# Attention and two dense stages on one core: the first batch's dense steps in two rounds of five inner blocks

## The chip, the cores and the metric

The kernel runs on one core of a Trainium2 chip. The metric is the device time of one execution, in microseconds; lower is better. Times of several executions are given by their median. Five engines run their own instruction streams in order and wait for each other by semaphores: TensorE (PE, matrix products and transposes), VectorE (DVE), ScalarE (ACT), GpSimd (POOL), and SyncE (SP), which here only issues DMA transfers.

## The reference, cut to what matters

```python
def _attn_ref(q, k, v, tau):                 # (4, 8, 576, 64) each
    scores = scale * np.matmul(q, k.transpose(0, 1, 3, 2))
    thresh = np.max(scores, axis=-1, keepdims=True) - tau
    scores = np.where(scores >= thresh, scores, -1000000000.0)
    attn = np.exp(scores - np.max(scores, axis=-1, keepdims=True))
    attn = attn / (np.sum(attn, axis=-1, keepdims=True) + 1e-09)
    return np.matmul(attn, v)
...
x = attn_out.transpose(0, 2, 1, 3).reshape(2304, 512)
h = x @ w_in                                 # moe: (512, 2048)
g = np.where(h >= 1, h, np.where(h <= -1, 0.0, (h + 1) ** 2 / 4))
x = g @ w_out                                # (2048, 512)
h = x @ w_in2                                # moe2
out = (h * np.clip(h + 3.0, 0.0, 6.0) / 6.0) @ w_out2
```

The result is compared in float32.

## The kernel before, in words

**Attention.** There are 16 jobs, one for each batch (4) and pair of heads (4); job j belongs to batch j // 4. A job has five blocks of 128 query rows (the last of 64) and one block is one step t of `attention()`, 80 steps in all. A step computes scores of two heads into two PSUM banks pairs, P0 and P1 (L285); VectorE reads them, negates them and finds the row maximum (L297); ScalarE takes the exponential (L301); VectorE applies the threshold and sums (L307). A step later TensorE transposes the result (L245, banks Q0, Q2 or Q3), ScalarE copies it to SBUF as `Gf` and `Gt` (L328, L342), and TensorE multiplies it with v (L362). Blocks 2, 3 and 4 of a job also hold the norm of the job before (L395 to L403) and the transposes of the next q and k (L257, L268), which take turns in the banks P0 and P1. The page's line L301 has nine instructions for each job, so the first of each nine marks a job's start.

**Dense stage 1 beside attention.** When the four jobs of batch 0 are done (in job 4, whose step t is 23), `dense1` begins to give out steps in the gaps of attention: for groups g of 256 tokens (two for each batch, six in all) and inner blocks f of 128, ten of the sixteen (NF1 = 10), a step n computes h for (g, f) (`em_h`, 12 products, L486; then ScalarE L495, L496, VectorE L497, ScalarE L503, GpSimd L504) and one or two parts of the outer product for an earlier step (`em_part`, 6 products each, L543, bank Q3). All matrices are split into a high and a low part of reduced float32, and three products are taken for each. `split_x` loads a group's activations (`xst`) and splits them (L469 on ScalarE, L470 on VectorE). The other six inner blocks follow after attention (L528), then stage 2.

**Weight conversions.** The dense weights come as 64-bit numbers and are converted in the kernel, 512 KB a block: 20 blocks (10 of w_in, 10 of w_out) are needed for `dense1`. A conversion has two halves. `split_a` is L111 and L114 on ScalarE, L115 on GpSimd, L122 on VectorE; `split_b` is L128 on VectorE, L130 on GpSimd, then the high part on GpSimd (L133) or, once `mode["mlp"]` is set, on ScalarE (L135), and the low part on GpSimd (L137). `Weights.prefetch` keeps three loads (`w_raw`) ahead of the conversion. From step t = 6 on, a half is emitted at each attention step, and a second at each even one; in `dense1`, `weights.upto` emits whatever is due two steps ahead by `first_use`.

**What sets the order.** A scheduler with its own clock orders each engine's instructions, moving those whose inputs are ready ahead of others; order is otherwise forced by `after(x, y)` alone, which keeps x behind y. In `split_a`, L111 is ordered behind `pins["S"]`, which is None during attention. TensorE's dense products are ordered behind the last but one attention product (`pin_mlp`).

Of the kernel before, what the change touches and what calls it, by code (L numbers as in the profile page):

```python
# [18 lines left out]
def kernel(  # L19
# [84 lines left out]
    def split_a(kind, m, f):  # L104
        t = wraw.pop((kind, m, f))
        pool = wbase if f < NF1 else wpool[f]
        hi = pool.tile([128, 512], F32R, tag=f"w{kind}h{f}", name=f"w{kind}h{f}")
        lo = pool.tile([128, 512], F32R, tag=f"w{kind}l{f}", name=f"w{kind}l{f}")
        c = stage.tile([128, 512], U32, tag="w_c", name="w_c", bufs=2)
        r = t[:, :, 0].bitcast(I32)  # L110
        x = S.activation(out=r, in_=t[:, :, 0], func=ACTF.Copy, scale=2.0 ** -29)  # L111
        after(x, pins["S"])
        if mode["att"]:
            S.activation(out=f32(c), in_=f32(t[:, :, 1]), func=ACTF.Abs)  # L114
            G.tensor_scalar(  # L115
                out=f32(c), in0=f32(c), scalar1=122879.9921875, scalar2=2.0 ** -15, op0=ALU.min, op1=ALU.max)
        else:
            S.activation(out=f32(c), in_=f32(t[:, :, 1]), func=ACTF.Abs)
            x = V.tensor_scalar(
                out=f32(c), in0=f32(c), scalar1=2.0 ** -15, scalar2=122879.9921875, op0=ALU.max, op1=ALU.min)  # L120
            after(x, pins["V"])
        V.tensor_scalar(out=c, in0=c, scalar1=3, scalar2=0x3FFFFFFF,  # L122
                        op0=ALU.logical_shift_left, op1=ALU.bitwise_and)
        wc[kind, m, f] = (hi, lo, c, t, r)
# [147 lines left out]
    def em_scores(j, i):  # L272
# [179 lines left out]
    def split_x(key, kks=range(KD)):  # L452
        m, g, ph = key
# [78 lines left out]
    def em_part(key, half, f):  # L532
# [3 lines left out]
        if f == 0:  # L536
            acc[key] = bank("Q3")
        a = acc[key]
        for i in range(2):
            c = slice((2 * half + i) * 128, (2 * half + i + 1) * 128)  # L540
            o = a[:, i * GRP:(i + 1) * GRP]
            for x, (l, r) in enumerate(((wh[:, c], gh), (wh[:, c], gl), (wl[:, c], gh))):
                mm = T.matmul(o, l, r, start=(f == 0 and x == 0 and i == 0),  # L543
                              stop=(f == NF1 - 1 and x == 2 and i == 1), skip_group_check=True)
# [4 lines left out]
        if f == NF1 - 1:  # L549
            ob = mt.tile([128, 512], F32, tag="io", name="ob", bufs=2)  # L550
            if half:
                S.activation(out=ob, in_=acc.pop(key), func=ACTF.Copy)
            else:
                V.tensor_copy(out=ob, in_=acc.pop(key))
            nc.sync.dma_start(
                out=narrow(x2p, key[1])[:, 2 * half:2 * half + 2, :],
                in_=ob.rearrange("p (k n) -> p k n", k=2))
# [34 lines left out]
    n_h = NG * NF1  # L592
    outs = [(g, half, f) for g in range(NG) for half in range(2) for f in range(NF1)]
    OFF = NF1 + 2 * MLAG - 3
    steps, o = [], 0
    while o < len(outs):
        n = len(steps)
        steps.append([])
        while o < len(outs) and (o < 2 * (n + 1) - OFF or n >= n_h) and outs[o][0] * NF1 + outs[o][2] + MLAG <= n:
# [4 lines left out]
    HOLD = 1 + max(n - g * NF1 - f for n, l in enumerate(steps) for g, half, f in l if half)  # L604

    def dense1(ready, ahead):

        for n, l in enumerate(steps[:n_h]):
            g, f = divmod(n, NF1)
            key = (0, g, 1)  # L610
            if key not in xs:
                while not ready(g):
                    yield None
                split_x(key)
            ahead(n, f)
# [221 lines left out]
```

## Time and profile before

| | us |
|---|---|
| median of 3 runs (1193.73 to 1196.18) | 1195.55 |
| the profiled execution | 1197.37 |
| its span, first to last instruction | 1195.6 |
| TensorE busy in it | 1139.7 (95%) |
| ScalarE busy | 628.8 (53%) |
| VectorE busy | 580.2 (49%) |
| GpSimd busy | 419.5 (35%) |

The shares are means over a program of several stages: attention alone, attention with dense steps from about 150 us, dense work alone from about 550 us. They say little of any one stage; the rows below cut the span by jobs.

### The profile page before, as it was taken

How to read it: one execution, taken by the hardware profiler on the slowest of the kernel's cores; microseconds unless marked ns; L12 is line 12 of the kernel's file. 1: busy time of each engine (PE TensorE's matmuls, PEld its weight loads, DVE VectorE, ACT ScalarE, POOL GpSimd, SP SyncE). 2: the span in 40 equal slices, each digit the busy share in tenths (PEclk: the TensorE clock that was granted, in tenths of full speed). 3: DMA queues.
4: the chain of work that ended last, by engine and by line, in shares of the span. 5: the costliest groups of instructions: out<-in, count | busy, mean ns of one | idle time of the engine just before them, and what ended most of it. 6: DMA issues, size and time to landing. Idle time of an engine off the chain costs nothing.

```text
span 1195.6 us, 17992 instructions
## 1 busy us (share of the span) xinstructions
PE 1139.7 (95%) x6680; PEld 908.8 (76%) x6680; DVE 580.2 (49%) x1196; ACT 628.8 (53%) x1218; POOL 419.5 (35%) x396
## 2 busy tenths in 40 slices
PE   6877789999999999999999999999999999999998
PEld 4444467776777777777888988888888888888886
DVE  4889865455565565653642675555740121121111
ACT  4677766564665665655654676654542222233222
POOL 1676621110111111112762666656742213222221
PEclk9989999999999999999999999999999999999999
DMA  4444521112211122103421244453210010010000
GB/s 119 125 126 135 146 59 40 50 42 60 61 28 39 52 59 68 30 20 112 154 89 44 85 136 158 144 166 99 89 46 12 1 58 9 1 44 2 18 1 36
DMA packets 106792, 82.45 MB, mean 69 GB/s; under 512 B 66512, under 2 KB 90576, under 8 KB 106704
## 3 DMA queue, kind: packets, MB, share of 16 engines
q1 hardware_dynamic: 105344, 81.00, 23.1%
q8 instruction: 53, 0.87, 0.3%
q10 hardware_dynamic: 1360, 0.30, 0.1%
q14 instruction: 35, 0.29, 0.1%
HBM read 63.96 MB, written 17.30 MB: 68 GB/s over the span
## 4 chain that ended last, share of the span: by engine, by line
PE 86%; DVE 5%; ACT 3%; DMA 3%; issue 1%; SPq 1%; POOL 1%; ACTq 0%; DVEq 0%; POOLq 0%
PE Q L486 34%; PE P L528 26%; PE Q L543 7%; PE Q L362 6%; PE P L285 6%; PE Q L245 5%; DVE p L297 2%; DMA w_raw<-in_moe_w_in_dram 1%; DVE p L307 1%; PE P L245 1%; ACT e L301 1%; DVE w_c L128 1%; DMA xd<-xu 1%; ACT r L495 0%; PE P L395 0%
## 5 line engine op out<-in xcount | busy, mean ns | idle before, releaser
L504 POOL TENSOR_TENSOR gl<-r,gh 128x512 fp32r<-128x512 f32 (+1 forms) x190 | 205.8, 1083 | 645.3 <-ACT gh L503 625.5
L486 PE MATMUL Q<-xh,wih 128*128 128x512 f32 (+1 forms) x760 | 265.1, 350 | 2.4 <-ACT xh L469 1.4
L486 PE MATMUL Q<-xl,wih 128*128 128x512 f32 (+1 forms) x760 | 257.8, 339 | 0.4 <-DVE xl L470 0.4
L486 PE MATMUL Q<-xh,wil 128*128 128x512 f32 (+1 forms) x760 | 257.4, 339 | 0.0
L500 DVE SCALAR_TENSOR_TENSOR r<-r,Q 128x512 f32<-128x512 f32 (+1 forms) x80 | 50.7, 633 | 248.4 <-ACT r L499 248.3
L486 PEld LDWEIGHTS Q<-xh,wih 128*128 128x128 f32 x760 | 144.6, 190 | 33.0 <-issue 10.6
L503 ACT ACTIVATE gh<-r 128x512 fp32r<-128x512 f32 (+1 forms) x190 | 99.9, 526 | 122.1 <-PE P L528 52.3
L486 PEld LDWEIGHTS Q<-xl,wih 128*128 128x128 f32 x760 | 144.5, 190 | 17.2 <-DVE xl L470 1.0
L486 PEld LDWEIGHTS Q<-xh,wil 128*128 128x128 f32 x760 | 144.3, 190 | 15.6 <-issue 0.5
L297 DVE TENSOR_SCALAR_CACHE_REDUCE p<-P 128x576 f32<-128x576 f32 x144 | 104.0, 752 | 82.7 <-PE Q L245 74.3
L307 DVE SCALAR_TENSOR_TENSOR p<-p,th,e 128x576 f32<-128x576 f32 x144 | 128.1, 904 | 21.8 <-ACT e L301 15.4
L245 PE MATMUL Q<-ident,p 128*128 128x128 f32 (+1 forms) x656 | 112.1, 284 | 16.6 <-DVE p L307 8.3
L301 ACT ACTIVATE e<-p,nm 128x576 f32<-128x576 f32 x144 | 109.6, 774 | 33.1 <-DVE p L297 31.9
L499 ACT ACTIVATE r<-Q,three 128x512 f32<-128x512 f32 (+1 forms) x80 | 51.4, 643 | 143.0 <-PE Q L486 139.9
L285 PE MATMUL P<-kt,qt 64*128 64x288 f32 (+1 forms) x640 | 107.2, 443 | 18.1 <-DVE p L297 11.3
L497 DVE SCALAR_TENSOR_TENSOR r<-r,Q 128x256 f32<-128x256 f32 (+1 forms) x110 | 55.1, 501 | 133.1 <-ACT r L496 131.5
L245 PEld LDWEIGHTS Q<-ident,p 128*128 128x128 f32 (+1 forms) x656 | 73.2, 141 | 57.9 <-issue 15.4
L528 PE MATMUL P<-woh,gh 128*128 128x512 f32 x288 | 111.9, 390 | 0.6 <-DVE ob L581 0.6
L528 PE MATMUL P<-wol,gh 128*128 128x512 f32 x288 | 112.2, 390 | 0.0
L528 PE MATMUL P<-woh,gl 128*128 128x512 f32 x288 | 111.0, 390 | 0.0
L130 POOL TENSOR_TENSOR w_c<-w_c,w_raw 128x512 int32<-128x512 int32 x64 | 89.4, 1397 | 44.1 <-DVE w_c L128 32.4
L328 ACT ACTIVATE Gf<-Q 128x512 f32<-128x512 f32 x128 | 75.3, 592 | 51.5 <-PE Q L245 51.3
(83 smaller groups left out, 1874.0 us busy)
## 6 DMA issues: line engine op xcount, KB each, us to landing
w_raw<-in_moe_w_in_dram SPq DMA_DIRECT2D x32, 512.0 KB, 4.0
w_raw<-in_moe_w_out_dram SPq DMA_DIRECT2D x32, 512.0 KB, 3.7
xst<-xd SPq DMA_DIRECT2D x28, 256.0 KB, 3.3
kn<-in_k_dram SPq DMA_DIRECT2D x32, 128.0 KB, 2.7
vn<-in_v_dram SPq DMA_DIRECT2D x32, 128.0 KB, 2.7
xd<-xu SPq DMA_DIRECT2D x16, 256.0 KB, 2.3
x2d<-ob SPq DMA_DIRECT2D x16, 256.0 KB, 3.6
xst<-x2d SPq DMA_DIRECT2D x16, 256.0 KB, 3.3
```

The source lines that it names most:

```text
L130: x = G.tensor_tensor(out=c.bitcast(I32), in0=c.bitcast(I32), in1=r, op=ALU.add)
L245: x = T.transpose(out, in_, ident)
L285: mm = T.matmul(o, qt[j][r, c], kt[j][r, k0:k0 + HS], start=True, stop=True, skip_group_check=True)
L297: V.tensor_scalar(out=p[:, x], in0=s[:, :, 0:HS], scalar1=-1.0, scalar2=3e38, op0=ALU.mult, op1=ALU.min, accum_out=nm[:, x:x + 1])
L301: S.activation(out=e, in_=p[:, x], func=ACTF.Exp, bias=nm[:, x:x + 1], scale=-1.0)
L307: V.scalar_tensor_tensor(out=p[:, x], in0=p[:, x], scalar=th[:, x:x + 1], in1=e, op0=ALU.is_le, op1=ALU.mult, accum_out=zt[j][:, z:z + 1])
L328: S.activation(out=f[:, h, :, d0:d0 + 128], in_=tm.rearrange("p (c n) -> p c n", c=4), func=ACTF.Copy)
L486: mm = T.matmul(h, l[:, kk * 128:(kk + 1) * 128], r, start=(x == 0), stop=(x == 3 * KD - 1))
L503: x = S.activation(out=gh, in_=r, func=ACTF.Copy)
L504: y = G.tensor_tensor(out=gl, in0=r, in1=f32(gh), op=ALU.subtract)
L528: T.matmul(a, l, r, start=(first and x == 0), stop=(last and x == 2))
L543: mm = T.matmul(o, l, r, start=(f == 0 and x == 0 and i == 0), stop=(f == NF1 - 1 and x == 2 and i == 1), skip_group_check=True)
```

## The change

It has three parts. `pins["S"]` now holds the newest exponential that was emitted, so L111 stays behind it, and L114 is ordered behind L111. The conversions ahead of the dense steps become five (`FIRST`): a half is emitted at steps 7, 8, 10, 11, and so on, until five are done; during `dense1`, `pace` emits halves up to 5 + 0.85 n conversions at step n, beside what `first_use` asks for. And groups 0 and 1 (batch 0) go through the ten inner blocks in two rounds of five: (g0, f 0-4), (g1, f 0-4), (g0, f 5-9), (g1, f 5-9). The second round loads the sums that the first has stored (`before`, L542 of the new file) and adds them on VectorE (L557) in place of a copy. Groups 2 to 5 are as they were.

```diff
-            S.activation(out=f32(c), in_=f32(t[:, :, 1]), func=ACTF.Abs)
+            after(S.activation(out=f32(c), in_=f32(t[:, :, 1]), func=ACTF.Abs), x)
...
-            S.activation(out=e, in_=p[:, x], func=ACTF.Exp, bias=nm[:, x:x + 1], scale=-1.0)
+            pins["S"] = S.activation(out=e, in_=p[:, x], func=ACTF.Exp, bias=nm[:, x:x + 1], scale=-1.0)
...
-        if f == 0:
+        g, fs = ROUNDS[key[3]]
+        dst = narrow(x2p, g)[:, 2 * half:2 * half + 2, :]
+        if f == fs[0]:
             acc[key] = bank("Q3")
+            if fs[0]:
+                before[key] = mt.tile([128, 512], F32, tag="before", name="before", bufs=1)
+                nc.sync.dma_start(out=before[key].rearrange("p (k n) -> p k n", k=2), in_=dst)
...
-        if f == NF1 - 1:
+        if f == fs[-1]:
             ob = mt.tile([128, 512], F32, tag="io", name="ob", bufs=2)
-            if half:
+            if key in before:
+                V.tensor_tensor(out=ob, in0=acc.pop(key), in1=before.pop(key), op=ALU.add)
+            elif half:
...
-    n_h = NG * NF1
-    outs = [(g, half, f) for g in range(NG) for half in range(2) for f in range(NF1)]
+    HALF = NF1 // 2
+    ROUNDS = [(g, list(range(f, f + HALF))) for f in (0, HALF) for g in range(2)]
+    ROUNDS += [(g, list(range(NF1))) for g in range(2, NG)]
+    before = {}
+    hs = [(r, f) for r, (g, fs) in enumerate(ROUNDS) for f in fs]
+    n_h = len(hs)
+    outs = [(r, half, f) for r, (g, fs) in enumerate(ROUNDS) for half in range(2) for f in fs]
...
-            for g, half, f in l:
-                yield from em_part((0, g, 1), half, f)
+            for i, (r, half, f) in enumerate(l):
+                if i == 1:
+                    pace(n + 0.5)
+                yield from em_part(round_key(r), half, f)
...
+    def pace(n):
+        goal = min(2 * len(by_use), 2 * FIRST + 2 * RATE * n)
+        while mode["att"] and 2 * weights.done + weights.mid < goal:
+            weights.half()
+
     def ahead1(n, f):
         weights.upto(sum(1 for x in by_use if first_use[x] < n + 2))
+        pace(n)
...
+    FIRST, RATE = 5, 0.85
...
-                weights.half()
-                if mode["t"] % 2 == 0:
+                if weights.done < FIRST and mode["t"] > 5 and mode["t"] % 3:
                     weights.half()
```

The order of the instructions moves at many places; three of them follow, each first as before and then as now.

ScalarE in job 0, from the copy of the first transposed scores on: `Gf` and `Gt` are those scores, `e` the exponential, `w_raw` and `w_c` a weight block in conversion. Before:

```order
L328 ACTIVATE Gf<-Q_230 128x4x128
L342 ACTIVATE Gt<-Q_260 128x128
L111 ACTIVATE w_raw<-w_raw 128x512
L114 ACTIVATE w_c<-w_raw 128x512
L111 ACTIVATE w_raw<-w_raw 128x512
L114 ACTIVATE w_c<-w_raw 128x512
L301 ACTIVATE e<-p,nm 128x576
L328 ACTIVATE Gf<-Q_263 128x4x128
```

Now:

```order
L328 ACTIVATE Gf<-Q_230 128x4x128
L342 ACTIVATE Gt<-Q_260 128x128
L301 ACTIVATE e<-p,nm 128x576
L328 ACTIVATE Gf<-Q_263 128x4x128
L328 ACTIVATE Gf<-Q_269 128x4x128
L342 ACTIVATE Gt<-Q_293 128x128
L301 ACTIVATE e<-p,nm 128x576 x3
```

Two conversions' first instructions stood between a copy and the third step's exponential; none stands there now, and none in the whole of job 0.

ScalarE in job 5, beside the dense steps, around the end of the job's fourth block: `r` and `gh` are a dense step's activation and its high part, `wih` a converted block's high part, `qt` the next q. Before:

```order
L342 ACTIVATE Gt<-Q_1819 128x128
L301 ACTIVATE e<-p,nm 128x576
L495 ACTIVATE r<-Q_1609,half 128x256
L301 ACTIVATE e<-p,nm 128x576
L496 ACTIVATE r<-r 128x256
L328 ACTIVATE Gf<-Q_1854 128x4x128
L257 ACTIVATE qt<-P_1949,taus 128x576
L503 ACTIVATE gh<-r 128x256
L328 ACTIVATE Gf<-Q_1866 128x4x128
```

Now:

```order
L342 ACTIVATE Gt<-Q_1813 128x128
L301 ACTIVATE e<-p,nm 128x576
L495 ACTIVATE r<-Q_1583,half 128x256
L301 ACTIVATE e<-p,nm 128x576
L135 ACTIVATE wih_1652<-w_c 128x512
L496 ACTIVATE r<-r 128x256
L328 ACTIVATE Gf<-Q_1848 128x4x128
L257 ACTIVATE qt<-P_1936,taus 128x576
L111 ACTIVATE w_raw<-w_raw 128x512
L503 ACTIVATE gh<-r 128x256
L328 ACTIVATE Gf<-Q_1863 128x4x128
L114 ACTIVATE w_c<-w_raw 128x512
```

The same attention and dense instructions stand in the same order, with three instructions of conversions among them.

VectorE at the same place of job 5: `p` and `nm` are the negated scores and their minimum, `th` the threshold, `r` the dense activation. Before:

```order
L297 TENSOR_SCALAR p,nm<-P_1903 128x576
L297 TENSOR_SCALAR p,nm<-P_1904 128x576
L304 TENSOR_SCALAR th<-nm,taus 128x2
L307 SCALAR_TENSOR_TENSOR p,z<-p,th,e 128x576 x2
L497 SCALAR_TENSOR_TENSOR r<-r,Q_1609 128x256
L297 TENSOR_SCALAR p,nm<-P_2007 128x576
L497 SCALAR_TENSOR_TENSOR r<-r,Q_1678 128x256
L304 TENSOR_SCALAR th<-nm,taus 128x1
L307 SCALAR_TENSOR_TENSOR p,z<-p,th,e 128x576
```

Now:

```order
L297 TENSOR_SCALAR p,nm<-P_1889 128x576
L297 TENSOR_SCALAR p,nm<-P_1890 128x576
L304 TENSOR_SCALAR th<-nm,taus 128x2
L307 SCALAR_TENSOR_TENSOR p,z<-p,th,e 128x576 x2
L122 TENSOR_SCALAR w_c<-w_c 128x512
L497 SCALAR_TENSOR_TENSOR r<-r,Q_1583 128x256
L128 SCALAR_TENSOR_TENSOR w_c<-w_raw,w_c 128x512
L297 TENSOR_SCALAR p,nm<-P_1983 128x576
L304 TENSOR_SCALAR th<-nm,taus 128x1
L497 SCALAR_TENSOR_TENSOR r<-r,Q_1691 128x256
L122 TENSOR_SCALAR w_c<-w_c 128x512
L307 SCALAR_TENSOR_TENSOR p,z<-p,th,e 128x576
```

L122 and L128 of two conversions now stand between the lines of attention and of the dense step.

## Rows read from the trace of the kernel before

**Rows 1.** Page, parts 1 and 2: busy us of each engine; TensorE in 40 slices

```profile
PE 1139.7 (95%) x6680; PEld 908.8 (76%) x6680; DVE 580.2 (49%) x1196; ACT 628.8 (53%) x1218; POOL 419.5 (35%) x396
...
PE   6877789999999999999999999999999999999998
```

**Rows 2.** Windows, jobs 0, 1-3, 2, 4-7: us, busy PE PEld DVE ACT POOL, clock

```profile
11.60:40.50 28.90, 19.33 (x118) 12.10 (x120) 21.20 (x54) 17.98 (x34) 11.44 (x12) 0.88 0.49 136
40.50:124.30 83.80, 64.31 (x409) 37.56 (x405) 76.19 (x164) 58.20 (x117) 57.01 (x56) 0.94 0.46 126
69.10:95.70 26.60, 20.78 (x135) 12.40 (x131) 26.08 (x57) 18.24 (x36) 17.95 (x16) 0.94 0.49 133
124.30:153.30 29.00, 22.06 (x139) 13.18 (x139) 26.77 (x60) 22.68 (x45) 18.61 (x16) 0.94 0.56 154
153.30:192.70 39.40, 37.95 (x280) 30.51 (x281) 20.03 (x55) 23.62 (x53) 7.02 (x10) 0.96 0.17 45
192.70:230.20 37.50, 36.55 (x272) 28.24 (x270) 21.06 (x58) 23.17 (x52) 5.53 (x8) 1.00 0.18 48
230.20:265.00 34.80, 34.66 (x259) 26.82 (x259) 19.07 (x54) 21.93 (x47) 5.11 (x7) 1.00 0.17 43
```

**Rows 3.** Chain that ended last, within 11.6 to 153.3 us, shares by line

```profile
by line: DMA w_raw<-in_moe_w_in_dram 12.5%; DVE p L307 12.4%; DVE p L297 10.6%; issue 7.9%; PE Q L362 7.0%; ACT e L301 4.6%; DVE w_c L128 4.4%; PE P L285 4.1%; PE Q L245 3.3%; POOL w_c L130 3.1%; DVE w_c L122 2.9%; DMA w_raw<-in_moe_w_out_d
...
18.19 5.17 DMA w_raw<-in_moe_w_in_dram
```

**Rows 4.** Waits of TensorE, 11.6 to 153.3 us: total us, times, longest

```profile
PE Q L245 <- DVE p L307: 8.3, 9, 1.8
PE P L285 <- DVE p L297: 7.5, 6, 2.0
PE Q L362 <- ACT Gf L328: 7.0, 4, 5.6
```

**Rows 5.** Waits of ScalarE, the same stretch

```profile
ACT w_raw L111 <- DMA w_raw<-in_moe_w_in_dram: 13.4, 8, 4.3
ACT w_raw L111 <- DMA w_raw<-in_moe_w_out_dram: 7.3, 5, 2.6
```

**Rows 6.** Timeline of ScalarE in job 0: start, us, instruction, idle before it

```profile
11.65 1.45 ACT L301 ACTIVATE e<-p,nm 128x576 f32<-128x576 f32 x2 [2.13 <-DVE p L297]
14.95 1.51 ACT L301 ACTIVATE e<-p,nm 128x576 f32<-128x576 f32 x2 [1.85 <-DVE p L297]
...
21.88 0.65 ACT L111 ACTIVATE w_raw<-w_raw 128x512 int32<-128x512 uint32 x1 [4.28 <-DMA w_raw<-in_moe_w_in_dram]
...
24.51 0.76 ACT L301 ACTIVATE e<-p,nm 128x576 f32<-128x576 f32 x1
```

**Rows 7.** Groups by line, 40.5 to 124.3 us: count, busy us, mean ns, idle before

```profile
L307 DVE SCALAR_TENSOR_TENSOR p<-p,th,e 128x576 f32<-128x576 f32 x27 | 29.5, 1104 | 4.0 <-ACT e L301 3.4
...
L130 POOL TENSOR_TENSOR w_c<-w_c,w_raw 128x512 int32<-128x512 int32 x13 | 18.8, 1447 | 21.6 <-DVE w_c L128 19.9 <-DVE z L379 1.7
...
L128 DVE SCALAR_TENSOR_TENSOR w_c<-w_raw,w_c 128x512 uint32<-128x512 uint32 x13 | 9.8, 756 | 0.0
...
L122 DVE TENSOR_SCALAR w_c<-w_c 128x512 uint32<-128x512 uint32 x13 | 9.5, 730 | 0.3 <-POOL w_c L115 0.3
L114 ACT ACTIVATE w_c<-w_raw 128x512 f32<-128x512 f32 x14 | 9.4, 671 | 0.8 <-POOL wol L137 0.8
...
L111 ACT ACTIVATE w_raw<-w_raw 128x512 int32<-128x512 uint32 x12 | 8.2, 684 | 10.6 <-DMA w_raw<-in_moe_w_out_dram 7.3 <-DMA w_raw<-in_moe_w_in_dram 3.3
...
L135 ACT ACTIVATE woh<-w_c 128x512 fp32r<-128x512 f32 x1 | 0.6, 616 | 0.0
```

**Rows 8.** The same view, 153.3 to 265 us (jobs 5 to 7)

```profile
L307 DVE SCALAR_TENSOR_TENSOR p<-p,th,e 128x576 f32<-128x576 f32 x27 | 22.0, 835 | 3.9 <-ACT e L301 2.5
...
L470 DVE TENSOR_TENSOR xl<-xst,xh 128x256 fp32r<-128x256 f32 x6 | 2.6, 464 | 3.8 <-ACT xh L469 3.7
...
L469 ACT ACTIVATE xh<-xst 128x256 fp32r<-128x256 f32 x6 | 2.3, 416 | 2.2 <-PE Q L486 2.2
```

More of the change, by code (lines that the diff above doesn't have):

```diff
@@ L452, in split_x @@
     def split_x(key, kks=range(KD)):
-        m, g, ph = key
+        m, g, ph = key[:3]
         r = xs.setdefault(key, [])
@@ L542, in em_part @@
             for x, (l, r) in enumerate(((wh[:, c], gh), (wh[:, c], gl), (wl[:, c], gh))):
-                mm = T.matmul(o, l, r, start=(f == 0 and x == 0 and i == 0),
-                              stop=(f == NF1 - 1 and x == 2 and i == 1), skip_group_check=True)
+                mm = T.matmul(o, l, r, start=(f == fs[0] and x == 0 and i == 0),
+                              stop=(f == fs[-1] and x == 2 and i == 1), skip_group_check=True)
                 if x == 0:
@@ L554, in em_part @@
                 V.tensor_copy(out=ob, in_=acc.pop(key))
-            nc.sync.dma_start(
-                out=narrow(x2p, key[1])[:, 2 * half:2 * half + 2, :],
-                in_=ob.rearrange("p (k n) -> p k n", k=2))
+            nc.sync.dma_start(out=dst, in_=ob.rearrange("p (k n) -> p k n", k=2))
     pbs = {}
@@ L598 @@
         steps.append([])
-        while o < len(outs) and (o < 2 * (n + 1) - OFF or n >= n_h) and outs[o][0] * NF1 + outs[o][2] + MLAG <= n:
+        while o < len(outs) and (o < 2 * (n + 1) - OFF or n >= n_h) and hs.index(outs[o][::2]) + MLAG <= n:
             steps[-1].append(outs[o])
@@ L603, with round_key @@
                 break
-    HOLD = 1 + max(n - g * NF1 - f for n, l in enumerate(steps) for g, half, f in l if half)
+    HOLD = 1 + max(n - hs.index((r, f)) for n, l in enumerate(steps) for r, half, f in l if half)
+    def round_key(r):
+        return (0, ROUNDS[r][0], 1, r)
     def dense1(ready, ahead):
         for n, l in enumerate(steps[:n_h]):
-            g, f = divmod(n, NF1)
-            key = (0, g, 1)
+            r, f = hs[n]
+            key = round_key(r)
             if key not in xs:
-                while not ready(g):
+                while not ready(key[1]):
                     yield None
@@ L616, in dense1 @@
             yield from em_h(key, 0, f)
-            if f == NF1 - 1:
+            if f == ROUNDS[r][1][-1]:
                 xs.pop(key)
-                if g + 1 < NG and ready(g + 1):
-                    split_x((0, g + 1, 1))
+                if r + 1 < len(ROUNDS) and ready(ROUNDS[r + 1][0]):
+                    split_x(round_key(r + 1))
             if n == n_h - 3 and not mode["att"]:
@@ L630, in behind @@
         for l in steps[n_h:]:
-            for g, half, f in l:
-                for _ in em_part((0, g, 1), half, f):
+            for r, half, f in l:
+                for _ in em_part(round_key(r), half, f):
                     pass
```

## The prediction, made before the result was known

> **What bounds the kernel now.** I began with the page's busy times and slices: TensorE is busy 1139.7 of 1195.6 us, and the slices below 9 tenths lie almost all in the first fifth of the span [rows 1]. So no edit can take more than the 56 us that TensorE idles, and it must do so at the front. A program made of 16 attention jobs is best cut at the first exponential of each job [rows 2]. Jobs 0 to 4 (11.6 to 153.3 us) take 28.9, 83.8 (three jobs) and 29.0 us. TensorE is busy for only 64.31 of the 83.8, VectorE (third pair of a row) for 76.19, and in job 2 VectorE is busy 26.08 of 26.60 us. Jobs 5 to 7, which carry dense steps too, are the reverse: TensorE 37.95 of 39.40, 36.55 of 37.50, 34.66 of 34.80. The bound changes sides at 153 us.
>
> The chain of waits over jobs 0 to 4 names what is late [rows 3]: weight loads 12.5% of 141.7 us, that is 17.7 us, then VectorE's two attention lines L307 and L297 with 23%, then the VectorE and GpSimd lines of the conversions (L128, L130, L122) with 10.4%. TensorE's own list of waits agrees: 8.3 us for L307, 7.5 for L297, 7.0 for Gf [rows 4]. ScalarE, which feeds both, stood 13.4 + 7.3 = 20.7 us in L111, the first instruction of a conversion, until a load had landed [rows 5]. One case in full: the exponentials run at 11.65 and 14.95 us, 3.3 us apart, the next is due near 18.5, but L111 stands ahead of it in ScalarE's queue, waits 4.28 us for its load until 21.88, two conversions follow, and the exponential starts at 24.51 [rows 6]. That is 6 us lost behind an instruction that nobody needed yet.
>
> **The change part by part.** (1) **Conversions leave the front.** By ScalarE's order, jobs 0 to 4 of the kernel before issue 5, 4, 4, 4, 4 conversions; after it 0, 2, 1, 2, 4, and jobs 5 to 7 take 6, 3, 2, where there were none. One conversion costs ScalarE 0.684 + 0.671 us, and 0.62 more for the high part once dense steps run; VectorE 0.730 + 0.756; GpSimd 1.447 and more [rows 7]. VectorE pays a second time: L307 averages 1.104 us in jobs 1 to 3 [rows 7] and 0.835 in jobs 5 to 7, which have no conversions [rows 8]; 27 x 0.269 / 13 = 0.56 us per conversion.
>
> Job 0: the 6 us above go, and nothing but attention is left; I take 28.9 to 23.5, **-5.4** (bounds -7, where it runs at TensorE's busy time plus a tenth, and -4, where part of the 6 us was cover for the loads of q and k). Jobs 1 to 3: 12 conversions become 5. VectorE's load falls by 7 x (1.49 + 0.56) = 14.3 us over three jobs, from 25.4 to 20.6 a job. TensorE is then the fuller engine with 21.4 a job (64.3 in the three jobs [rows 2], slow-clock stretches included; the granted clock there is 0.94, so 1.7 us of a job is lost to it). The measured 83.8 us cannot fall below 3 x 21.4 = 64; an engine that waits for two others for its banks does not run full, and I take 87% busy, 24.6 a job, 74 us, **-9.8**. The near end is 27 a job (-3), the far end 22.3 (-17), TensorE as full as in job 5. Job 4 keeps its four conversions and loses only part of the high parts and the two early pieces of the next stage: **-1** (-3 to 0).
>
> (2) **The order on ScalarE.** The pin puts L111 behind the newest exponential and L114 behind L111. It costs no instruction. What queues behind L111 on ScalarE is the copy of the transposed scores (L328), and TensorE's L362 waits for that; with three loads asked for ahead and about 16 us between conversions in the front, a load, for which ScalarE waited 4.3 us at the longest [rows 5], has landed long before. I put the pin itself at 0; its gain is in (1).
>
> (3) **Conversions enter the dense part.** The pace of 0.85 conversions a step is not what sets it: the table of first uses still says that inner block f is due at step f, so 15 of the 20 are done by step 8, and job 5 gets six. ScalarE there: 23.6 us busy now; added 6 x (0.684 + 0.671 + 0.62) = 11.9, and 4 x 0.416 for one more split of the activations [rows 8], together 13.5: at most 37.1 of 39.4 us (neighbours on ScalarE overlap a little, so their sum is a ceiling). VectorE: 20.0 + 6 x 1.49 + 6 x 0.56 + 4 x 0.464 = 34.2. Both still fit under TensorE's 38, at 94 and 87%; VectorE ran at 98% in job 2 and set the pace there. So the work hides, but no longer freely, and an exponential or a copy that stands behind 2 us of conversion now makes TensorE wait. I take **+2.5** for job 5 (0 to +8; the far end is four waits like those of the front's jobs 1 to 3, 2 us each). Job 6, with 3 (and five high parts and one more split): ScalarE 23.2 + 8.8 of 37.5, **+0.5** (0 to +3). Job 7, with 2: **0** (0 to +1.5).
>
> GpSimd's part of this is where a rule can be weighed. In the rows L307 grows by 0.56 us per conversion, far less than GpSimd works on one. The Trainium skill, "SBUF — State Buffer", section "Who interferes with whom", says that a VectorE instruction with two SBUF inputs and a GpSimd instruction that reads SBUF exclude each other, and that the later one blocks fully, not partly. Taken at its full price, one L130 of 1.447 us per conversion, VectorE in job 5 would need 34.2 + 6 x 0.89 = 39.5 us, as much as the job lasts; the job would then grow by about 5 instead of 2.5 and the whole gain would be 10 and not 12.5. I keep the row's 0.56, since it holds for the same two instructions under a fuller VectorE.
>
> (4) **Two rounds.** 60 inner steps and 120 outer parts stay, so TensorE's work is the same. New are two splits of activations (4 loads, 8 L469, 8 L470), four loads of a partial sum with four VectorE adds in place of copies, and four more hand-overs of the one accumulator bank. The loads read what was stored some five steps (over 25 us) earlier and wait for nothing recent; on SP's queue they stand ahead of loads of q, k and v by a few places. Each split and hand-over is covered by attention work on TensorE; I give **+0.7** (0 to +2).
>
> Sum: -5.4 - 9.8 - 1 + 2.5 + 0.5 + 0.7 = **-12.5 us** (bounds -27 and +7.5). The profiled execution took 1197.4 us, 1.8 of it outside its span, and would take 1184.9; the median of the runs is 1195.55, so I forecast **1183.0**.
>
> **The rivals.** *The score banks bind next.* A step's scores fill both pairs of banks, and the next step's scores wait until L297 has read them; q, k and the norm take turns in the same banks. For it: 7.5 us of TensorE's waits in the front are on L297 [rows 4], and L297 has to run twice a step whatever else leaves the queue. Against it: the first steps, with no conversion about, run 3.3 us apart [rows 6], and VectorE is so full today that L297 mostly waits for its turn. If it holds, jobs 1 to 3 fall by 1 us each: -5.4 - 3 - 1 + 3.7 = -5.7, **1190**. *The dense part hides everything* and the front runs as full as job 5: -7 - 16.3 - 3 + 0.7 = -25.6, **1170**; for it that ScalarE is at 60% in job 5 today, against it that every conversion is a chain over three engines that all carry attention work. *ScalarE becomes the bound behind 153 us* (the slower one): each of the 11 conversions in jobs 5 to 7 puts its 1.97 us on the path, because TensorE issues in order and its transposes and products wait for ScalarE's copies, and L111 waits for its load as it does today, 20.7 / 21 = 1 us each: 11 x 3 = 33 against the front's -16.2, +0.7 for the rounds: +17, **1212**. It decides from 15.5 / 11 = 1.4 us per conversion on. For it: six conversions fall into one job. Against it: VectorE carries 98% in job 2 and its job is not longer than the others, and the pin keeps the wait for a load from standing ahead of an exponential.
>
> **How the numbers follow.** The forecast has 0.57, the score banks 0.20, all hidden 0.15, ScalarE bound 0.08. About 0.2% (2.4 us) is what a measurement of this kernel can tell from no change. The forecast's own spread, 1176 to 1191, is faster but for 0.02; the banks rival gives 0.15 faster and 0.05 same; all hidden is faster; ScalarE bound is slower. Faster 0.85, same 0.06, slower 0.09. The range reaches from the all-hidden case to the edge of no gain, where jobs 1 to 3 hardly fall: 1170 to 1196.
>
> **What would show it.** Right: no wait for a load ahead of an exponential at 18 us; job 0 at 23 to 25 us; jobs 1 to 3 near 24.6 with VectorE below 21 and TensorE the fuller engine; the first dense step some 15 us earlier; job 5 at 39 to 45 us with ScalarE at 35 to 37. Jobs 8 and later unchanged. Wrong: jobs 1 to 3 at 27 with L297 as TensorE's longest wait (banks), or job 5 over 50 us with TensorE waiting for L328 or L301 (ScalarE bound), or a loss behind 265 us, which nothing here explains.

## The result: 1182.0 us, about 1% faster, with two errors that nearly cancel

The changed kernel takes 1182.02 us (median of 4 runs, 1181.79 to 1185.07) against 1195.09 for the kernel before (4 runs). The ratio is 0.9897, with a 95% interval of 0.9878 to 0.9917. The forecast was 1183.0. The profiled execution took 1181.81 us against 1197.37.

Page of the changed kernel, span and busy times (as in [rows 1]):

```profile
span 1180.0 us, 17986 instructions
PE 1133.5 (96%) x6680; PEld 907.5 (77%) x6680; DVE 581.4 (49%) x1208; ACT 631.2 (53%) x1234; POOL 412.3 (35%) x388
```

No engine's work changed by more than 2%. The time went elsewhere, and the windows by jobs say where. Columns are those of [rows 2]: stretch, length, then busy time of PE, PEld, DVE, ACT and POOL, and the granted clock. The rows are jobs 0, 1 to 3, 2, 4, 5, 6 and 7; the last, from an answer on the whole stretch, is jobs 5 to 7 together:

```profile
10.90:29.60 18.70, 16.67 (x112) 11.04 (x112) 15.14 (x44) 12.81 (x25) 0.77 (x2) 0.91 0.57 152
29.60:101.10 71.50, 62.62 (x419) 38.09 (x421) 57.21 (x151) 49.29 (x103) 20.45 (x23) 0.98 0.32 86
52.70:75.90 23.20, 19.48 (x127) 11.64 (x124) 20.05 (x51) 14.34 (x28) 5.79 (x7) 0.95 0.39 109
101.10:125.00 23.90, 20.04 (x143) 12.98 (x139) 22.69 (x54) 18.61 (x37) 9.89 (x11) 1.00 0.48 131
125.00:170.30 45.30, 37.59 (x253) 28.84 (x254) 34.31 (x72) 34.40 (x76) 31.44 (x32) 0.92 0.40 115
170.30:212.60 42.30, 39.14 (x296) 31.20 (x295) 29.88 (x69) 30.25 (x69) 20.49 (x21) 1.00 0.43 125
212.60:250.00 37.40, 34.12 (x253) 26.20 (x253) 25.20 (x61) 25.75 (x55) 13.26 (x14) 1.00 0.34 101
...
125.00:250.00 125.00, 110.85 (x798) 86.24 (x799) 89.39 (x200) 90.40 (x197) 65.19 (x66) 0.97 0.40 114
```

| stretch | before, us | after, us | moved | forecast (bounds) |
|---|---|---|---|---|
| up to job 0 | 11.6 | 10.9 | -0.7 | none |
| job 0 | 28.9 | 18.7 | -10.2 | -5.4 (-7 to -4) |
| jobs 1 to 3 | 83.8 | 71.5 | -12.3 | -9.8 (-17 to -3) |
| job 4 | 29.0 | 23.9 | -5.1 | -1 (-3 to 0) |
| jobs 5 to 7 | 111.7 | 125.0 | +13.3 | +3.0 (0 to +12.5) |
| the rest of the span | 930.6 | 930.0 | -0.6 | +0.7 (0 to +2) |

The sum is -15.6 us in the profiled executions and -13.1 in the medians. The front gave 28 us where 16 were forecast, and the part beside the dense steps took back 13 where 3 were forecast. The total is right to 1 us, but job 0, job 4 and jobs 5 to 7 lie outside their bounds; of the last, job 5 grew by 5.9 us (bounds 0 to 8), job 6 by 4.8 (0 to 3) and job 7 by 2.6 (0 to 1.5). TensorE's own work is little of the 13.3: it is busy for 110.85 us there, and was for 109.16 [rows 2]; the rest is time in which it waits. The experiments ask why.

Two more views answer to rows shown ahead. ScalarE's timeline in job 0 (as in [rows 6]) has no load between the exponentials; the third step's now starts at 17.65 us, 3.3 after the second's:

```profile
14.30 1.51 ACT L301 ACTIVATE e<-p,nm 128x576 f32<-128x576 f32 x2 [1.96 <-DVE p L297]
...
17.65 0.78 ACT L301 ACTIVATE e<-p,nm 128x576 f32<-128x576 f32 x1 [0.70 <-DVE p L297]
```

TensorE's waits in jobs 0 to 4, 10.9 to 125 us (as in [rows 4]: total, times, longest):

```profile
PE Q L245 <- DVE p L307: 5.3, 6, 1.0
PE P L285 <- DVE p L297: 3.3, 4, 1.5
...
PE Q L362 <- ACT Gf L328: 1.2, 3, 0.5
```

and in jobs 5 to 7, 125 to 250 us:

```profile
PE Q L245 <- ACT Gf L328: 8.0, 3, 3.6
PE Q L486 <- DVE r L497: 3.2, 3, 1.6
```

where the longest before, in jobs 5 to 7 (153.3 to 265 us), was

```profile
PE P L285 <- DVE p L297: 3.1, 2, 2.8
```

The list has moved from the front to the dense part, and there it names the copies that ScalarE makes of transposed scores (L328) and VectorE's line of the dense step (L497).

### The profile page after: what moved, and what is told of

It reads as the page before. It is cut to its first block, busy times and chain, and to the rows that moved or that the text cites. A ratio compares the mean times of both kernels' runs of the same rounds, so it can differ in the third digit from the quotient of the medians.

```text
span 1180.0 us, 17986 instructions
## 1 busy us (share of the span) xinstructions
PE 1133.5 (96%) x6680; PEld 907.5 (77%) x6680; DVE 581.4 (49%) x1208; ACT 631.2 (53%) x1234; POOL 412.3 (35%) x388
## 4 chain that ended last, share of the span: by engine, by line
PE 82%; ACT 5%; DVE 5%; DMA 4%; issue 2%; POOL 1%; ACTq 0%; SPq 0%; DVEq 0%; POOLq 0%
PE Q L486 33%; PE P L528 26%; PE Q L548 6%; PE Q L362 6%; PE P L285 5%; PE Q L245 5%; DVE p L297 2%; ACT e L301 1%; DVE p L307 1%; DMA xst<-xd 1%; PE P L245 1%; DMA xd<-xu 1%; ACT Gf L328 1%; DMA w_raw<-in_moe_w_out_dram 1%; ACT r L495 1%
## 5 line engine op out<-in xcount | busy, mean ns | idle before, releaser
L297 DVE TENSOR_SCALAR_CACHE_REDUCE p<-P 128x576 f32<-128x576 f32 x144 | 104.1, 754 | 70.8 <-PE Q L245 54.3
L307 DVE SCALAR_TENSOR_TENSOR p<-p,th,e 128x576 f32<-128x576 f32 x144 | 125.5, 886 | 25.0 <-ACT e L301 18.3
L497 DVE SCALAR_TENSOR_TENSOR r<-r,Q 128x256 f32<-128x256 f32 (+1 forms) x110 | 55.0, 500 | 119.0 <-ACT r L496 118.5
L285 PE MATMUL P<-kt,qt 64*128 64x288 f32 (+1 forms) x640 | 103.7, 432 | 10.3 <-DVE p L297 4.4
L130 POOL TENSOR_TENSOR w_c<-w_c,w_raw 128x512 int32<-128x512 int32 x64 | 90.5, 1414 | 39.8 <-DVE w_c L128 33.2
L328 ACT ACTIVATE Gf<-Q 128x512 f32<-128x512 f32 x128 | 75.0, 590 | 47.6 <-PE Q L245 47.4
```

Source lines behind the costliest of these rows:

```text
L130: x = G.tensor_tensor(out=c.bitcast(I32), in0=c.bitcast(I32), in1=r, op=ALU.add)
L285: mm = T.matmul(o, qt[j][r, c], kt[j][r, k0:k0 + HS], start=True, stop=True, skip_group_check=True)
L297: V.tensor_scalar(out=p[:, x], in0=s[:, :, 0:HS], scalar1=-1.0, scalar2=3e38, op0=ALU.mult, op1=ALU.min, accum_out=nm[:, x:x + 1])
L307: V.scalar_tensor_tensor(out=p[:, x], in0=p[:, x], scalar=th[:, x:x + 1], in1=e, op0=ALU.is_le, op1=ALU.mult, accum_out=zt[j][:, z:z + 1])
L328: S.activation(out=f[:, h, :, d0:d0 + 128], in_=tm.rearrange("p (c n) -> p c n", c=4), func=ACTF.Copy)
```

## The experiments

They compare with the kernel before, run beside them (1195.05 to 1195.21 us), and with the changed kernel's 1182.0.

### One: the pin alone

```diff
-            S.activation(out=e, in_=p[:, x], func=ACTF.Exp, ...)
+            pins["S"] = S.activation(out=e, in_=p[:, x], func=ACTF.Exp, ...)
...
-            S.activation(out=f32(c), ..., func=ACTF.Abs)
+            after(S.activation(out=f32(c), ..., func=ACTF.Abs), x)
```

> The kernel before with one part of the change: the first instruction of a conversion stays behind the newest exponential, and the second behind the first. By ScalarE's order jobs 0 to 7 then hold 0, 4, 4, 4, 2, 6, 0, 0 conversions (before: 5, 4, 4, 4, 4, 0, 0, 0). Theory (what is saved is VectorE's and ScalarE's load of conversions in jobs 1 to 3, and the waits only in job 0): job 0 near 19 us, jobs 1 to 3 still 27 to 28 us each, job 5 some 45 us; in all 1184 to 1190 us. Rival (what hurt was a load waited for ahead of an exponential, the place and not the load of the engines): jobs 1 to 3 fall to 24 us with the same 12 conversions, and the whole is at 1172 to 1178 us.

`split_b` orders the high part L135 behind the same `pins["S"]`, so the pin holds L135 back too, which the description of the change leaves out.

Measured: 1192.05 us, ratio 0.9971 (0.9958 to 0.9984); one of the ten executions took 2243.64 us, and nothing here has a cause for it. Windows of job 0 and of jobs 1 to 3:

```profile
10.90:30.00 19.10, 16.91 (x112) 11.11 (x112) 15.14 (x44) 12.81 (x25) 0.78 (x2) 0.91 0.56 149
30.00:115.70 85.70, 68.38 (x415) 40.54 (x417) 72.25 (x163) 56.85 (x118) 50.97 (x51) 0.89 0.42 115
```

The total lies 2 us above the theory's range, but its statements on job 0 and jobs 1 to 3 hold nearly: job 0 takes 19.1 us, so the pin alone gives nearly all of that term, by keeping every conversion out of the job; jobs 1 to 3 stay slow, at 28.6 each, with the same 12 conversions, pinned or not. ScalarE's waits in L111 for loads, 10.6 us in jobs 1 to 3 before [rows 7], are gone here, and these jobs are no faster for it. The rival falls: neither the place in ScalarE's queue nor the loads made jobs 1 to 3 slow. Between 12 conversions (85.7 us) and 5 (71.5) a conversion costs 14.2 / 7 = 2.0 us there; 5.8 of the 14.2 us are TensorE's own busy time (68.38 against 62.62), at a granted clock of 0.89 against 0.98.

### Two: everything but the pin

```diff
-            after(S.activation(out=f32(c), ..., func=ACTF.Abs), x)
+            S.activation(out=f32(c), ..., func=ACTF.Abs)
...
-            pins["S"] = S.activation(out=e, in_=p[:, x], func=ACTF.Exp, ...)
+            S.activation(out=e, in_=p[:, x], func=ACTF.Exp, ...)
```

> The changed kernel without the pin (five conversions in front and two rounds stay as written). By ScalarE's order the scheduler then brings all 20 conversions back into jobs 0 to 3, five each. Theory (the place of the conversions makes the gain): jobs 0 to 3 at 27 to 29 us as before, jobs 5 to 7 as before, and the two more seams of the rounds cost 1 to 4 us: 1195 to 1200 us. Rival (the number emitted in front and the rounds make it): at most 1185 us.

Measured: 1202.71 us, ratio 1.0064 (1.0045 to 1.0082): slower than the kernel before, and by 3 us more than the range said. Windows of jobs 1 to 3 and of jobs 5 to 7:

```profile
39.00:130.90 91.90, 68.68 (x414) 41.16 (x416) 77.42 (x169) 66.74 (x137) 58.16 (x57) 0.89 0.46 129
156.70:269.00 112.30, 110.45 (x807) 85.10 (x807) 63.59 (x174) 71.56 (x159) 17.99 (x25) 1.00 0.23 63
```

The rival falls. `FIRST = 5` and the pace say when a conversion is written down, not when it runs; without the pin the scheduler fills the front with all 20. Jobs 5 to 7, now with the two rounds but no conversions, take 112.3 us against 111.7 before: the rounds' own seams cost next to nothing.

### Three: no rounds

```diff
-    ROUNDS = [(g, list(range(f, f + HALF))) for f in (0, HALF) for g in range(2)]
-    ROUNDS += [(g, list(range(NF1))) for g in range(2, NG)]
+    ROUNDS = [(g, list(range(NF1))) for g in range(NG)]
```

> The changed kernel with batch 0 in one round of ten inner blocks, as before. By ScalarE's order conversions are 0, 2, 1, 2, 4, 7, 4, 0 in jobs 0 to 7 (with rounds 0, 2, 1, 2, 4, 6, 3, 2). Theory (the price is paid for each conversion beside dense work, wherever it falls, and the rounds' seams cost 2 to 4 us): 1178 to 1183 us. Rival (the rounds are needed, since 11 conversions crowded into jobs 5 and 6 make TensorE wait): 1187 us or more.

Measured: 1183.11 us, ratio 0.9886 (0.9858 to 0.9915), with single runs from 1179.1 to 1185.7. That cannot be told from the changed kernel. The rival, by which the rounds are needed, falls; that they cost 2 to 4 us isn't shown either (the second run speaks against it). The largest piece of the diff does nothing that these runs can measure. By `first_use` the inner blocks are still due in the old order, which may be why; no run changes that alone.

### Four: a staging buffer for the activations alone

```diff
-                    t = mt.tile([128, 2, GRP], F32, tag="io", name="xst", bufs=2)
+                    t = mt.tile([128, 2, GRP], F32, tag="xst", name="xst", bufs=1)
...
-            ob = mt.tile([128, 512], F32, tag="io", name="ob", bufs=2)
+            ob = mt.tile([128, 512], F32, tag="io", name="ob", bufs=1)
```

> The changed kernel with a staging buffer of its own for the activations that are loaded for a split (one buffer) and one for the sums that are stored (one), in place of two that both take in turn. In the changed kernel's trace a split at 172 us waits 4.5 us for a sum's store to leave the shared buffer, then 2.9 us for its load, and TensorE stands 2.9 us. Theory (that seam costs about 3 us of the 13.5 that jobs 5 to 7 lost): job 6 some 3 us shorter, 1178 to 1180 us. Rival (the wait only moves, since a single buffer makes the second half of a split wait for the first): 1181 to 1185 us.

Measured: 1183.0 us, ratio 0.9895 (0.9879 to 0.9911); job 6 is 41.9 us against 42.3. The theory falls, and the total is in the rival's range. The changed kernel's ScalarE timeline, where TensorE stood 2.9 us, shows what the theory left out: the long idle time ahead of the copy L328 is before L135, which waits for GpSimd's L130:

```profile
172.66 0.40 ACT L503 ACTIVATE gh<-r 128x256 fp32r<-128x256 f32 x1
174.52 0.78 ACT L469 ACTIVATE xh<-xst 128x256 fp32r<-128x256 f32 x2 [1.45 <-PE Q L486]
177.83 0.63 ACT L135 ACTIVATE wih<-w_c 128x512 fp32r<-128x512 f32 x1 [2.54 <-POOL w_c L130]
...
180.19 0.57 ACT L328 ACTIVATE Gf<-Q 128x512 f32<-128x512 f32 x1
```

The split's second half (L469) starts after that, at 179.25 us, when its load has landed, and ScalarE stands only 0.42 us for it. The two waits lie side by side ahead of L328: to take away the load's alone moves the copy by 0.4 us at most.

### Five to seven: parts of the later conversions left out

The 15 conversions after the fifth (`LATE`) lose all of their work, then only VectorE's and GpSimd's, then only GpSimd's.

```diff
+        if (kind, m, f) in LATE:      # whole: load_w, split_a and split_b return here
+            return
...
-            G.tensor_scalar(out=f32(c), in0=f32(c), ..., op0=ALU.min, op1=ALU.max)
+            if (kind, m, f) not in LATE:   # without GpSimd; L130 and L137 likewise
+                G.tensor_scalar(out=f32(c), in0=f32(c), ..., op0=ALU.min, op1=ALU.max)
```

> The changed kernel with the 15 conversions after the fifth left out, their loads too (the dense steps take the first converted block in their place). Theory (the 13.5 us that jobs 5 to 7 grew by are the price of conversions beside dense work): jobs 5 to 7 return to the 111.6 us that they took in the kernel before, job 4 to 22, the whole to 1166 to 1170 us. Rival (a good part is the price of the two rounds, whose seams stay here): 1173 to 1177 us.

> The same 15 conversions with their loads and ScalarE's three instructions kept, and VectorE's and GpSimd's left out. Theory (ScalarE pays: its own 2 us each, and its waits for loads ahead of the copies that TensorE needs): 1177 to 1182 us. Rival (VectorE's and GpSimd's part of the chain pays): within 3 us of the run without the 15 conversions, at most 1172 us.

> The same 15 conversions with loads, ScalarE's and VectorE's instructions kept and GpSimd's three to four left out. Theory (ScalarE pays): no more than 2 us faster than the changed kernel, 1180 to 1182 us. Rival (GpSimd is what makes the price, by holding L307 back and by the low parts of dense steps that queue behind it): 1170 to 1175 us.

Measured: 1171.56 us without the conversions (0.9802, 0.9785 to 0.9819), 1175.09 with loads and ScalarE's part (0.9831, 0.9813 to 0.9849), 1172.37 with all but GpSimd's part (0.9808, 0.9792 to 0.9824). The first lies between the two ranges given for it (jobs 5 to 7 take 109.2 us, less than the theory's 111.6, but job 4 takes 24.9 and not 22), the second in neither of its ranges, the third in its rival's. Windows of jobs 5 to 7, in this order:

```profile
128.10:237.30 109.20, 107.31 (x791) 82.84 (x791) 63.64 (x173) 70.15 (x156) 17.61 (x24) 1.00 0.23 63
```

```profile
127.50:243.30 115.80, 111.60 (x808) 86.20 (x808) 63.87 (x174) 86.95 (x192) 16.93 (x25) 0.99 0.38 111
```

```profile
126.80:241.70 114.90, 111.34 (x806) 85.81 (x805) 74.91 (x196) 87.41 (x193) 16.80 (x25) 0.99 0.40 115
```

The 15 conversions cost 10.5 us by the medians (1182.0 - 1171.6). ScalarE did nearly as much in the third run as in the changed kernel, 87.41 us busy against 90.40, with the same loads, and by the medians the price is nearly gone: GpSimd's part of 3.4 us a conversion makes 9.7 of the 10.5 us. In jobs 5 to 7 alone it makes less of more: they take 109.2 us without the conversions, 114.9 without GpSimd's part and 125.0 with all, so GpSimd's part makes 10.1 of 15.8 us, and 5.7 stay with loads, ScalarE and VectorE. The totals hide most of these 5.7: job 5 begins 1.3 us earlier in the third run than in the first, and what follows job 7 is 2.4 us shorter. So ScalarE is not the one that pays most, neither as I put it in the forecast nor in these expectations. VectorE shows the trace of GpSimd's part: 74.91 us busy in the third run, 89.39 in the changed kernel, with 196 and 200 instructions.

The second run does less than the third and is 2.7 us slower. The scheduler made another order of each; so some 3 us is what an order alone can do here, and smaller differences between such kernels are not read as effects.

### Eight: two conversions in front

```diff
-    first_use = {("i", f): f for f in fs1}
+    first_use = {("i", f): min(n for n, (r, x) in enumerate(hs) if x == f) for f in fs1}
...
-    FIRST, RATE = 5, 0.85
+    FIRST, RATE = 2, 0.85
```

> The changed kernel with two conversions in front in place of five, and with the inner blocks' due steps taken from the rounds; by ScalarE's order conversions are 0, 2, 0, 0, 4, 6, 6, 2 in jobs 0 to 7. Theory (a conversion costs 2.0 us in jobs 1 to 3, by the kernel with the pin alone against the changed one: (85.6 - 71.5) / 7, and 13.5 / 11 = 1.2 beside dense steps): 3 x 0.8 = 2.4 us faster than the changed kernel, 1178 to 1181 us. Rival (the price beside dense steps rises with their number, as ScalarE fills up): 1183 to 1187 us.

Measured: 1184.53 us, ratio 0.9899 (0.9873 to 0.9925), single runs from 1178.9 to 1185.8. Windows of jobs 1 to 3 and of jobs 5 to 7:

```profile
29.50:97.40 67.90, 59.49 (x411) 35.85 (x411) 52.17 (x145) 44.58 (x93) 11.32 (x14) 1.00 0.29 74
121.30:251.90 130.60, 116.09 (x798) 86.90 (x799) 96.71 (x206) 95.24 (x206) 77.25 (x75) 0.96 0.42 122
```

The front gives 3.6 us for three conversions fewer, 1.2 each and not the 2.0 between 12 and 5, and the dense part takes back 5.6. The next three cost some 1.9 us each there, where the first ones cost 1.2 (15.8 / 13). That the price beside dense steps rises with their number is not shown by this: three times 0.7 is less than an order alone can do, the due steps were changed too, and the profiled execution is the slowest of the four. The total is in the rival's range; from the changed kernel it can't be told.

### Nine: GpSimd's work set aside

GpSimd does instructions of the same shapes on two buffers of its own (`side`); no other engine reads them, and the later conversions do without GpSimd's part, as in run seven. `lastg` holds the newest low part of a dense step (ahead of the first one, a copy of a job's norm).

```diff
+            else:
+                after(G.tensor_scalar(out=side[0], in0=side[0], ..., op0=ALU.min, op1=ALU.max), lastg[0])
...
+            after(G.tensor_tensor(out=i[0], in0=i[0], in1=i[1], op=ALU.add), lastg[0])
+            after(G.tensor_tensor(out=side[0], in0=side[0], in1=side[1], op=ALU.subtract), lastg[0])
```

> As the run without GpSimd's part of the 15 later conversions (1172.4 us), but GpSimd does as much work of the same shapes on two buffers of its own, in its queue behind each dense step's low part, that nobody waits for. Theory (GpSimd's occupation is the price: it holds VectorE's two-input instructions back, and dense steps' low parts queue behind it): 1178 to 1183 us, L307 back to 1.0 us in jobs 5 to 7. Rival (the chain is the price: ScalarE's third instruction waits for GpSimd's result, and the load buffers come free only when GpSimd has read them): 1171 to 1175 us.

Measured: 1186.46 us, ratio 0.9928 (0.9911 to 0.9945). The window of jobs 5 to 7:

```profile
128.10:254.30 126.20, 115.70 (x805) 88.01 (x805) 95.70 (x196) 87.67 (x193) 69.59 (x70) 0.97 0.36 105
```

and the threshold line (L307 of the kernel before) in the same jobs, first the changed kernel, then run seven without GpSimd, then this one, each of the last two with a small VectorE line (L304 of the kernel before) under it; columns are busy us, mean ns, idle before:

```profile
L307 DVE SCALAR_TENSOR_TENSOR p<-p,th,e 128x576 f32<-128x576 f32 x27 | 27.2, 1025 | 4.9 <-ACT e L301 4.2
```

```profile
L316 DVE SCALAR_TENSOR_TENSOR p<-p,th,e 128x576 f32<-128x576 f32 x27 | 22.0, 833 | 2.7 <-ACT e L310 1.9
...
L313 DVE TENSOR_SCALAR th<-nm,taus 128x2 f32<-128x2 f32 x12 | 2.7, 225 | 0.2
```

```profile
L326 DVE SCALAR_TENSOR_TENSOR p<-p,th,e 128x576 f32<-128x576 f32 x27 | 29.8, 1125 | 2.3 <-ACT e L320 1.4
...
L323 DVE TENSOR_SCALAR th<-nm,taus 128x2 f32<-128x2 f32 x12 | 8.9, 743 | 0.2
```

The rival, by which the chain through GpSimd's results is the price, falls as the main cause: work that nobody waits for costs 14 us against run seven. It is more than the changed kernel's 9.7, and above the range, where GpSimd did 15 such threes in these jobs and the changed kernel 13 conversions. VectorE is where it shows: the threshold line grows from 833 to 1125 ns with nothing changed but GpSimd's being busy. One instruction of GpSimd and two of this line, from the run's timeline (start, us):

```profile
184.39 1.27 POOL L137 TENSOR_TENSOR side<-side,side 128x512 int32<-128x512 int32 x1
...
184.44 1.84 DVE L326 SCALAR_TENSOR_TENSOR p<-p,th,e 128x576 f32<-128x576 f32 x1
...
186.21 0.81 DVE L326 SCALAR_TENSOR_TENSOR p<-p,th,e 128x576 f32<-128x576 f32 x1
```

The mean of 1125 ns is two kinds. Of the 27 threshold instructions, 12 start while an instruction of GpSimd runs; each of them ends 0.61 to 0.62 us after the end of that instruction and takes 0.98 to 1.84 us. The other 15 take 0.80 to 0.82. VectorE's L297, which reads its scores from PSUM, is not lengthened: 14 of its instructions start inside one of GpSimd's, and all take about 0.75 us. In the changed kernel 7 threshold instructions of 27 start so and take 1.06 to 1.86 us; one more, of 1.94 us, starts 0.03 us ahead of one of GpSimd's, and the others take 0.80 to 0.82.

How the lengthened lines reach TensorE is less plain. Its waits for VectorE's dense line (L497 of the kernel before) grow, first run seven, then this one:

```profile
PE Q L495 <- DVE r L506: 0.4, 1, 0.4
```

```profile
PE Q L505 <- DVE r L516: 4.4, 4, 2.4
```

In the changed kernel it is the wait for ScalarE's copy L328 that leads, 8.0 us, and run four shows one such wait behind the chain through GpSimd's L130. So GpSimd's occupation alone is enough for such a price; what share the chain has in the changed kernel's own 9.7 us stays open. Nor does the run separate GpSimd's hold on VectorE from the dense steps' low parts that queue behind it on GpSimd; TensorE's waits for that queue are 0.4 us in all, as in run seven.

### Ten and eleven: GpSimd's work moved to VectorE

```diff
-        x = G.tensor_tensor(out=lo, in0=f32(c), in1=f32(hi), op=ALU.subtract)
-        after(x, pins["G"])
+        if mode["att"] and mode["mlp"]:
+            V.tensor_tensor(out=lo, in0=f32(c), in1=f32(hi), op=ALU.subtract)
+        else:
+            x = G.tensor_tensor(out=lo, in0=f32(c), in1=f32(hi), op=ALU.subtract)
+            after(x, pins["G"])
...
-            G.tensor_scalar(                                # run eleven only
+            (V if mode["mlp"] else G).tensor_scalar(
```

> The changed kernel with the low part of a conversion computed on VectorE in place of GpSimd once dense steps run; all work is done. Theory (GpSimd makes the price, VectorE has room at 34 of 45 us): 1.35 of GpSimd's 3.4 us a conversion go, 2 to 4 us faster than the changed kernel, 1177 to 1180 us. Rival (VectorE's 0.7 us more per conversion delay the attention as much): 1182 to 1186 us.

> The same with the clamp (the first of GpSimd's instructions) on VectorE too, where it takes some 0.4 us by the VectorE line L122 of the same kind. Theory: GpSimd keeps 1.4 of 3.4 us a conversion, 4 to 7 us faster than the changed kernel, 1175 to 1178 us. Rival (VectorE fills up): 1182 us or more.

Measured: 1180.26 us with the low part on VectorE (0.9873, 0.9855 to 0.9891), 1187.13 with the clamp there too (0.9936, 0.9915 to 0.9957). The first lies 0.3 us above the theory's range and is the fastest kernel of this study that does all its work, though its interval overlaps the changed kernel's. The second is slower than both: job 4 takes 30.8 us and job 5 50.0. TensorE waits 4.5 us there for VectorE's L497, so VectorE's queue has a part in it; why one instruction of some 0.4 us costs so much more than its length isn't settled.

### Twelve: the front without GpSimd

```diff
+            if f >= NF1 or m or kind + str(f) == "i0":     # L130, L133, L137 likewise
                 G.tensor_scalar(out=f32(c), in0=f32(c), ..., op0=ALU.min, op1=ALU.max)
```

> The kernel with the pin alone (1192.1 us; 4, 4, 4 conversions in jobs 1 to 3, which take 85.6 us), with GpSimd's part of all conversions but the first left out. Theory (GpSimd makes the price in the front too): jobs 1 to 3 at 72 to 76 us, the whole at 1176 to 1181 us. Rival (VectorE's own two instructions and ScalarE's two make it): jobs 1 to 3 at 81 us or more, the whole at 1186 us or more.

Measured: 1179.61 us, ratio 0.9863 (0.9840 to 0.9887). The window of jobs 1 to 3, and the threshold line there, in this run and in the kernel with the pin alone:

```profile
30.00:107.90 77.90, 65.77 (x419) 39.08 (x421) 62.02 (x165) 56.70 (x118) 7.42 (x10) 0.93 0.46 127
```

```profile
L315 DVE SCALAR_TENSOR_TENSOR p<-p,th,e 128x576 f32<-128x576 f32 x27 | 21.9, 818 | 5.0 <-ACT e L309 3.7
```

```profile
L307 DVE SCALAR_TENSOR_TENSOR p<-p,th,e 128x576 f32<-128x576 f32 x27 | 27.7, 1046 | 4.1 <-ACT e L301 3.1
```

Jobs 1 to 3 fall to 77.9 us, between the two ranges; the total is in the theory's. GpSimd's part of 12 conversions is worth 7.8 us there. Of the 14.2 us between 12 conversions and 5, seven conversions' GpSimd work would be 4.5, a third (if it goes by number); the other two thirds stay with the loads and with ScalarE's and VectorE's own instructions, which no run separates in the front. There both theories hold a share.

## Why the prediction was right, and where only its sum was

**What bounds the kernel** was read rightly in the main: jobs 1 to 4 by VectorE, jobs 5 to 7 by TensorE. The loads waited for, which the forecast names beside VectorE, cost time in job 0; in jobs 1 to 3 they cost nothing that shows, by run one. The gain came from the front, and nothing behind 250 us moved.

**Job 0** (-5.4, measured -10.2) was mis-sized, not misread. The term took back one stall of 6 us. But in job 0 VectorE lost the work of five conversions too (21.20 us busy before, 15.14 after), and that was not counted. Its far bound failed as well, "TensorE's busy time plus a tenth": that busy time, 19.33 us in [rows 2], holds 118 products at a granted clock of 0.88, over a job that the stalls had stretched; with the conversions away it is 112 products, 0.91 and 16.67 us. A busy time from a stretch that is itself disturbed is no floor. Run one shows that the pin alone gives 9.8 of the 10.2 us.

**Jobs 1 to 3** (-9.8, measured -12.3) came as worked out: TensorE is busy for 62.62 of 71.50 us, 88%, where 87% was taken, and VectorE fell to 57.21 us, 19.1 a job, where 20.6 was forecast. Runs one and twelve show both parts of the working, the engines' own load and GpSimd's hold.

**Job 4** (-1, measured -5.1): I counted starts of conversions, four in each kernel. But GpSimd's busy time fell from 18.61 to 9.89 us; in the changed kernel most of those conversions start late in the job, and their second halves run in job 5. Run five, with no conversion in job 4, takes 24.9 us there against 23.9: what is left of them in the job costs nothing that shows. A conversion is to be counted where its costly engine works.

**Jobs 5 to 7** (+3.0, measured +13.3) was the step that failed most, and in it jobs 6 and 7 (+0.5 forecast, +7.4 measured) more than job 5. The count of conversions was right, and so was ScalarE's load: at most 37.1 us was forecast for job 5, 34.40 was measured; VectorE's 34.2 against 34.31. Neither engine was full. What failed is the step from there, that work which fits beside TensorE's hides but for a few waits. What the runs put in its place: GpSimd's part makes most of what the conversions cost, 9.7 of 10.5 us by the medians and 10.1 of 15.8 in these jobs. It lengthens VectorE's instructions (run nine), and holds ScalarE's L135 ahead of a copy (run four); how much of the price goes either way isn't shown. I had priced it at 0.56 us per conversion, as extra busy time of an engine that had room; run nine shows that this time is paid in waits although there is room. A mean over L307 alone also missed other lines that grow: in jobs 5 to 7 VectorE's busy time differs by 14.5 us between the changed kernel and run seven, of which L307 is 5.2; two more conversions that fall into the window are some 2.3 (L122 and L128 at run seven's 0.43 and 0.74 us).

This is the place where a rule was weighed against a row. The Trainium skill, "SBUF — State Buffer", section "Who interferes with whom", has the later of the two engines block fully. The instructions of run nine agree with that, one by one; the row's 0.56 us is a mean over some that are blocked and others that are not. As prices, each was right in one thing. VectorE's busy time in job 5 came out by the row's (34.31 us; 34.2 by the row, 39.5 by the rule's full price, which supposes one full block for each conversion). The job's growth of 5.9 us was nearer to the 5 of the full price than to 2.5, but not for the reason given with it, a VectorE as full as the job: it is busy for 34.31 of 45.30 us.

**The pin at 0** in itself: in job 0 it is nearly the whole gain, but by moving conversions out, which was counted under the first part. Run two shows that without it nothing of the change works. **The rounds** at +0.7: nothing measurable, as runs two and three show.

**The rivals.** The score banks do not bind: TensorE's wait for L297 fell from 7.5 to 3.3 us. The dense part does not hide everything. (The sum of that rival takes -16.3 for jobs 1 to 3, where TensorE as full as in job 5 gives the -17 of the far end; 1170 becomes 1169.) ScalarE as the main bound behind 153 us is ruled out by run seven. The slower rival had the right place, and the price per conversion (1.2 us) came near the 1.4 us at which it would decide, but mostly by another engine.

So the total was right because a gain of 12 us too little stood against a loss of 10 us too little. That they cancelled is luck: no step of the forecast ties one to the other. What they share is that a conversion was priced too low wherever it stands (for each one that moved, 1.1 us in job 0 against 2.0 measured, 1.4 against 1.8 in jobs 1 to 3, and 0.3 against 1.2 in jobs 5 to 7); job 4's 4 us come from a wrong count instead.

## What to carry to other kernels

Where a scheduler orders the instructions, a rule on when work is written down does nothing unless something pins it: first look at where the work stands in the queues. Price background work by taking it away whole on the chip, not by the busy time that it adds: an engine at 70% can still pay in waits. And a term's floor must come from an undisturbed stretch; a right sum of terms that are each mis-sized proves none of them. And a mean over a line that is blocked at times hides what a block costs: look at its single instructions.

## What the hardware showed unexpectedly

GpSimd's instructions of 0.8 to 1.4 us on buffers that no other engine touches lengthened VectorE's threshold line from a mean of 833 to 1125 ns, and a VectorE instruction on two columns (L304 of the kernel before, 225 ns in run seven) to a mean of 743 ns. Of the twelve on two columns, nine start while an instruction of GpSimd runs, and each ends 22 to 32 ns after it; the longest of the nine takes 1.24 us. Two of the other three take 0.22 and 0.23 us; the third, of 1.34 us, starts 0.03 us ahead of one of GpSimd's.
